# Attention beside a gated MLP on one core: which key tiles VectorE takes, and the lengths a build-time order is made from

## The chip, the core and the metric

One core of a Trainium2 chip runs the whole kernel. TensorE multiplies (its results land in PSUM, eight banks of 128 x 512 float32), ScalarE evaluates exp and gelu, VectorE and GpSimd work elementwise, and DMA queues move data between memory and the on-chip SBUF. Each engine executes its own list of instructions in order; where one needs another's result it waits for a semaphore. The metric is the device time of one execution in microseconds. Five executions of the kernel before took 743.12, 743.48, 743.58, 744.07 and 745.52 us, so the median is 743.58.

## The reference, cut to what matters

`x` has 2048 rows of 512. `a` is attention with 32 heads of width 16 that share one set of keys and values; `b` is a gated MLP whose second half is layer-normalised and multiplied by a 2048 x 2048 matrix. A sigmoid gate per row mixes them.

```
q = (x @ wq) as 32 heads of 16;  k = x @ wk;  v = x @ wv
p = softmax(q k^T * 0.25);       a = (p v, heads side by side) @ wo
z = gelu(x @ w_in);              z1, z2 = halves of z, 688 columns each
g = w_sp @ layernorm(z2) + b_sp; b = (z1 * g) @ w_out
out = s * a + (1 - s) * b,       s = sigmoid(sum(x * gate_w))
```

The costly part is the softmax: 32 heads x 2048 queries x 2048 keys are 134 million exponentials.

## The kernel before, in words

**Attention blocks.** The work on scores is cut into 32 units (`NU`). A unit is one chunk of 512 queries (there are four) with four heads, and has 16 key tiles of 128 keys; a block is one key tile of one head, a 128 x 512 tile of scores. So there are 32 x 16 x 4 = 2048 blocks, and each passes through one matmul on TensorE (`s_mm`, shown by the profile as `ps<-QA,KA`), an exponential, and one matmul with the values (`ps<-P,V` or `ps<-X,V`) that accumulates into one PSUM bank for the unit.

**Two engines make the exponentials.** ScalarE takes two blocks at a time: TensorE fills one of two pairs of banks (0 and 1, 2 and 3), and one ACTIVATE turns the 128 x 1024 scores into P (`exp_op`, L621). VectorE takes a whole key tile of a unit, four blocks, which the code calls a batch. It drains two blocks at a time from banks 4 and 5 with a linear map (`d_A`, L645, two drains for each batch), then squares the 128 x 2048 result twice (`d_square`, L657). The fourth power of a linear function stands in for exp, and what it misses is a linear function of the scores, which eight short matmuls for each unit put back (`cor_mm`, with the sums MC and CC made once by `g_MC`, L451). MC is built for the last 1, 2, ... up to `NMAX` = 7 key tiles, since a unit's VectorE tiles are taken from the end of its list of tiles. GpSimd does a share of the second square: up to two pieces of `GE` = 384 columns of a batch (`g_piece`, L664), and VectorE's second square is shorter by as much.

**The start.** x arrives transposed in four chunks of 512 rows. For each chunk, TensorE multiplies by wk (`g_K`, L357) and VectorE copies the keys out of PSUM (`k_ev`, L350); `g_V` (L412) makes values, the gate's sums and a second copy of the keys (L418 to L420). After the keys of the last chunk, four DMAs issued by GpSimd copy all keys to other partitions (`k_shift`, L352 to L354); units with an odd number need that copy. Key tile n belongs to chunk n // 4. In the kernel before, ScalarE goes through the key tiles 0, 1, 2, ... and VectorE takes 15, 14, 13, ...; so VectorE's first tile needs the last chunk of keys (`new_batch`, L791, asks for `("K", 0, 3)`).

**The rest.** The MLP (`g_z2`, `z1_mm`, `g_sp`, `g_fin`, `g_part`) fills what TensorE and VectorE have left between the attention steps; the gelus run on ScalarE in one stretch of their own, between two table loads. The groups of such matmuls share one PSUM bank (`BM`), which VectorE empties. At the end the last unit is normalised and four row tiles are written out (L1302 to L1311). `keep_pick` (L1045) puts matmuls whose result adds nothing where TensorE had little to do for 3.4 us.

**The order.** All of these instruction lists are made while the kernel is built, by a planner that plays the engines forward with a fixed length for each piece of work (`pe_pick` L854, `act_pick` L1110, `dve_pick` L1157, main loop from L1258). The lengths that matter here: `LAT` = 120 ns from an engine's end to what another sees of it, `EXPT` = 904 ns for an exp of two blocks, `C512` = 218 ns for a 512-column matmul, `SW` = 105 ns when TensorE changes from one kind of matmul to another, 226 ns for a step of scores. TensorE may begin a step of scores once the exp two steps back has ended and must begin it `SLATE` = 490 ns before the running exp ends (`dl`, L918); other matmuls are only placed if they end before that. A pair of blocks for VectorE is placed `LAT + DMARG` = 220 ns after the last drain has ended (`d_ok`, L838). The times decide only the order; on the chip the semaphores decide when things run.

```
ACT's blocks of a unit, in order:   order = [(n // 4, n % 4) for n in range(64)]
VectorE's next key tile:            un["hi"] -= DB;  batches.append((u, un["hi"] // 4))
latest begin of a step of scores:   dl = max(t, nxt - SLATE)
```

Of the kernel before, what the change touches and what calls it, by code (L numbers as in the profile page):

```python
# [17 lines left out]
DH = 16  # L18
# [12 lines left out]
K2MAX = 0.142  # L31
ZMAX = 25.0

NPB = 21
NX = 6
DB = 4
NQ = 4
NMAX = 7
# [4 lines left out]
DPQ = 3500.0  # L43
SOLO = 300.0
PJOIN = 1
APRI = 1.5
DMARG = 100.0
DRAW = 115.0
RIDE = 0.0
GE = 384  # L50
GLAT = 160.0
GNS = (60.0, 2.0)
EMARG = 50.0
EXPT = (0, 478, 904, 1330)
SLATE = 490.0
KEEP = 7.5
LOW = 6.5
MMARG = 120.0
# [109 lines left out]
def build_kernel(nc, x_d, wq_d, wk_d, wv_d, wo_d, win_d, wsp_d, bsp_d, wout_d, gw_d, out_d):  # L168
    es = ExitStack()
    with es:  # L170
# [22 lines left out]
        wvg = sb("wvg", [128, 4, 34], B16)  # L193
# [123 lines left out]
        BMK = ("bk", BM)  # L317
        T = {"now": 0.0}
        LAT = 120.0
        C512, C344 = 218.0, 148.0  # L320
        SW = 105.0
        C2 = 78 + 0.5208 * 256 * DB

        class Group:
# [87 lines left out]
        def g_V(c):  # L412
            def piece(k, dt):
                t0 = 512 * c + 128 * k
                return lambda: mm(bank(BM, 33, 64 * k), xT[:, dt, t0:t0 + 128], wvg[:, dt, 0:33], dt == 0, dt == 3,
                                  ["wv", "gw", "wvk", ("x", c)], [BMK], tag="V")
            src = bank(BM, 256).rearrange("p (k w) -> p k w", w=64)
            e1 = lambda: op("dve", lambda v: v.tensor_copy(V1[:, 4 * c:4 * c + 4, 0:DH], src[:, :, 0:DH]), r=[BMK], w=[("V", c)], tag="Vev")  # L418
            e2 = lambda: op("dve", lambda v: v.tensor_copy(gs[:, 4 * c:4 * c + 4].unsqueeze(2), src[:, :, 32:33]), r=[BMK], w=[("gs", c)], tag="gsev")
            e3 = lambda: op("dve", lambda v: v.tensor_copy(KT0[:, 4 * c:4 * c + 4, :], src[:, :, 16:32]), r=[BMK], w=[("KT0", c)], tag="ktev")  # L420

            def done(t):
                T[("V", c)] = t
                if c >= 2:
                    dve_q.append((600, lambda: op("dve", lambda v: v.tensor_copy(
                        Kt[:, 4 * (c - 2):4 * (c - 2) + 4, :].rearrange("p k (h d) -> p k h d", d=DH),
                        KT0[:, 4 * c:4 * c + 4, :].unsqueeze(2).broadcast_to([128, 4, 8, DH])), r=[("KT0", c)], w=[("Kt", c)], tag="Kt"), t, setT(("Kt", c))))
                if c == 3:
                    gate_and_k()
            def all_():  # L430
                for k in range(4):
                    for dt in range(4):
                        piece(k, dt)()
            return Group("V%d" % c, [(480, all_)], [(150, e1), (100, e2), (130, e3)],
                         lambda: when(("x", c)), done)

        def gate_and_k():
            t = T["now"] + 400
# [12 lines left out]
        def g_MC():  # L451
            pieces = []
            for h in range(2):
                for i in range(NMAX):
                    kt = 15 - i
                    pieces.append((90, lambda h=h, i=i, kt=kt: mm(
                        bank(BM, 32 * (NMAX - i), 256 * h + 32 * i).rearrange("p (n e) -> p n e", e=32),
                        Kt[:, kt - 8, :] if h == 0 else ones[:, 0:128], V1[:, kt, :].unsqueeze(1).broadcast_to([128, NMAX - i, 32]),
                        i == 0, i == NMAX - 1, [("Kt", kt // 4), ("V", kt // 4), "ones"], [BMK], tag="MC")))
            msrc = bank(BM, 32 * NMAX).rearrange("p (n e) -> p n e", e=32).unsqueeze(2).broadcast_to([128, NMAX, 8, 32])  # L460
            mk = mke[:].unsqueeze(1).unsqueeze(3).broadcast_to([128, NMAX, 8, 32])
            e1 = lambda: op("dve", lambda v: v.tensor_tensor(MC[:], msrc, mk, ALU.mult), r=[BMK, "mke"], w=["MC"], tag="MC")
            e2 = lambda: op("dve", lambda v: v.tensor_scalar(ct[:, 0, :], bank(BM, 32 * NMAX, 256), E0, None, ALU.mult), r=[BMK], w=["ct0"], tag="CC")
            cc = CC[:, :, :].rearrange("p n e -> p (n e)")
            e3 = lambda: op("dve", lambda v: v.tensor_copy(cc, ct[:, 0, :]), r=["ct0"], w=["CC"], tag="CC")
            e4 = lambda: op("dve", lambda v: v.tensor_tensor(ct[:, 1, :], ct[:, 0, :], cc, ALU.subtract), r=["ct0", "CC"], w=["ct1"], tag="CC")
            e5 = lambda: op("dve", lambda v: v.tensor_scalar(ct[:, 1, :], ct[:, 1, :], s01[:, 1:2], None, ALU.mult), r=["ct1", "s01"], w=["ct1"], tag="CC")
            e6 = lambda: op("dve", lambda v: v.scalar_tensor_tensor(cc, cc, s01[:, 0:1], ct[:, 1, :], ALU.mult, ALU.add), r=["CC", "ct1", "s01"], w=["CC"], tag="CC")
            def some(h):
                for c_, f_ in pieces[NMAX * h:NMAX * h + NMAX]:  # L470
                    f_()
            return Group("MC", [(500, lambda: some(0)), (500, lambda: some(1))], [(1950, e1), (320, e2), (320, e3), (320, e4), (250, e5), (320, e6)],
                         lambda: when(("Kt", 2), ("Kt", 3), ("V", 2), ("V", 3)), setT("MC"))

        def g_RH():

# [255 lines left out]
        op("dve", lambda v: v.tensor_scalar(s01[:, 0:1], pidx[:, 0:1], 0.0, None, ALU.is_equal), r=["pidx"], w=["s01"])  # L732
        op("dve", lambda v: v.tensor_scalar(s01[:, 1:2], pidx[:, 0:1], 1.0, None, ALU.is_equal), r=["pidx"], w=["s01"])

        for c in range(4):
            T[("x", c)] = 6300.0 + 4200.0 * c
        T[("K", 0, 0)] = 8000.0
        T[("Q", 0)] = 9000.0
        T["wq1"] = 9000.0
        T["win"] = 29000.0  # L740
        T[("wT", 0)] = 55000.0
# [21 lines left out]
        misc = {"cur": None, "free": 0.0}  # L763

        units = [{"lo": 0, "hi": 64, "left": 64, "cor": 0} for _ in range(NU)]
        order = [(n // 4, n % 4) for n in range(64)]
        st_ = {"ua": 0, "kf": 0, "ke": 0, "pu": 0, "pp": 0}
        stepb, sdone, edone = {}, {}, {-1: 0.0, -2: 0.0}
        pfree = [0.0] * NPB
# [21 lines left out]
        def new_batch(now):  # L791
            m = len(batches)
            if m >= NX and pd_left.get(m - NX, 0) > 0:
                return False
            ua = unit_for_act()
            for u in (ua, ua + 1):
                if u >= NU:
                    continue
                un = units[u]
                if un["hi"] - un["lo"] < (RMIN if u < NU - 1 else RLAST) + DB or un["hi"] <= 64 - 4 * NMAX:  # L800
                    continue
                if u > ua and un["hi"] <= 64 - PRE:
                    continue
                q = when(("Q", u // 2), ("K", 0, 3)) if u % 2 == 0 else when(("Q", u // 2), "K1")
                if q is None or q > now:
                    continue
                un["hi"] -= DB
                batches.append((u, un["hi"] // 4))
                pd_left[m] = DB
                cur["m"] = m  # L810
                cur["hs"] = [0, 1]
                return True
            return False
# [22 lines left out]
            return take  # L836

        def d_ok(now):  # L838
            return dpair["free"] is not None and dpair["free"] + LAT + DMARG <= now and sum(1145 if x[1] == "dW" else 2290 for x in polyq) <= DPQ

        class Done(dict):
            def get(self, k):
# [6 lines left out]
        edone = Done(edone)  # L849

        def sw(kind):
            return 0.0 if last_pe["kind"] == kind else SW

        def pe_pick(now):  # L854
            k = st_["kf"]
# [21 lines left out]
                    cands.append((t + (0 if ph["j"] else LAT), 0, C512 + sw("M"), emit_z, fin_z, "M"))  # L877
            elif ua < NU and edone.get(k - 2) is not None:
                bl = []
                t = edone[k - 2] + (LAT if k >= 2 else 0)  # L880
                u = ua
                lo = units[u]["lo"]
                while len(bl) < 2 and u < NU:
# [14 lines left out]
                if bl:  # L898
# [12 lines left out]
                        unit_for_act()  # L911

                    def fin(t_end):
                        sdone[k] = t_end + LAT
                        for x in new:
                            da_q.append((t_end + LAT + EMARG,) + x)
                    nxt = edone[k - 1] if edone.get(k - 1) is not None else edone[k - 2] + (EXPT[len(stepb[k - 1])] if k - 1 in stepb else 0)
                    dl = max(t, nxt - SLATE)  # L918
                    ride = dpair["end"] + LAT + DMARG
                    if max(now, t) < ride <= dl - RIDE and (cur["hs"] or new_ok(now)):  # L920
                        t = ride
                    cands.append((t, 0, sw("S") + 226, emit, fin, "S"))
            if d_ok(now) and (dl is None or ua >= NU or t > now + SOLO):
                tk3 = d_pair(now, ())
                if tk3:
                    new3 = []

                    def fin_d(t_end):
                        da_q.append((t_end + LAT + EMARG,) + new3[0])
                    cands.append((now, 1, sw("S") + 216, lambda: new3.append(tk3()), fin_d, "S"))  # L930
            elif dpair["free"] is not None and dpair["free"] + LAT + DMARG > now:
                cands.append((dpair["free"] + LAT + DMARG, 9, 0, None, None))

            pu = st_["pu"]
            if pu < NU:
# [102 lines left out]
                cands = [c for c in cands if c[3] is None or c[5] == "S" or c[1] == 0.5 or max(now, c[0]) + c[2] <= dl]  # L1038
            return cands

        last_pe = {"kind": ""}
        tl_state = {12: 0, 13: 0}
        tl_bank = {12: BM, 13: BD}

# [65 lines left out]
        def act_pick(now):  # L1110
# [8 lines left out]
            if ph["k0"] is not None and gel and st_["ke"] == ph["k0"]:  # L1119
                kind, i = gel[0]  # L1120
                t = now if kind == "z2" else zready.get(i)
                if t is not None:
                    c_ = (1294 if kind == "z2" else 904) + (1300 if (kind, i) == ("z2", 0) or len(gel) == 1 else 0)

                    def e1():
                        gel.popleft()
# [133 lines left out]
        while True:  # L1260
# [5 lines left out]
            if rdy:  # L1266
# [6 lines left out]
                tend[eng] = t_end  # L1273
                if eng == "pe":
                    last_pe["kind"] = c[5]
                heapq.heappush(events, t_end)
                heapq.heappush(events, t_end + LAT)
                if c[4]:
# [198 lines left out]
```

## Time and profile before

| | |
|---|---|
| median of five executions | 743.58 us (743.12 to 745.52) |
| the profiled execution | 745.25 us, span from first to last instruction 743.3 us |
| ScalarE busy | 723.6 us, 97% of the span |
| VectorE busy | 699.8 us, 94% |
| TensorE busy | 697.0 us, 94% |
| GpSimd busy | 295.8 us, 40% |
| exps of two blocks on ScalarE | 760 |
| drains on VectorE | 264, for 132 batches |

The span is what the trace covers; the device time has 1.95 us more around it. A row of the groups names the source line, engine and operation, the tile written and the tiles read, the shape and the count, then the busy time in us, the mean length of one in ns, the idle time of that engine just before them, and what ended most of it. Because consecutive instructions of ScalarE and VectorE overlap a little in the records, the distance from start to start is shorter than the length of one: 904 ns against 1209 ns for the exps.

### The profile page before, as it was taken

The numbers are of one execution on the slowest core, as the hardware profiler recorded it, in microseconds if no ns is written. First come the engines' busy times: TensorE is split into PE (matmuls) and PEld (weight loads), VectorE is DVE, ScalarE is ACT, GpSimd is POOL, SyncE is SP. The second block draws the span as 40 slices with busy tenths as digits, with TensorE's granted clock in tenths as the row PEclk, the third lists the DMA queues.
The fourth block names the chain that finished last, engine by engine and source line by source line (L and its number), as shares of the span: only waits on it lengthen the run. The fifth ranks groups of instructions, "written<-read, shape, count | busy, mean of one in ns | idle before, by whom it ended". The sixth has DMA issues, their size and how long they took to land.

```text
span 743.3 us, 14057 instructions
## 1 busy us (share of the span) xinstructions
PE 697.0 (94%) x5502; PEld 186.0 (25%) x5502; DVE 699.8 (94%) x803; ACT 723.6 (97%) x786; POOL 295.8 (40%) x305
## 2 busy tenths in 40 slices
PE   7989999999899999999999999999999999999996
PEld 2322222223322222222222222222222222222221
DVE  3699999999999999999999999999999999999996
ACT  5999999999899999999999999999999999999995
POOL 4234433333134534434234444434444443444441
PEclk9999999999989999999999999999999999999999
DMA  9810000000000000140000042000005000000001
GB/s 214 179 25 1 1 1 1 1 1 1 1 1 1 1 1 2 30 94 22 1 1 1 1 86 52 8 1 1 1 1 114 15 8 9 1 1 1 1 1 33
DMA packets 49114, 17.06 MB, mean 23 GB/s; under 512 B 44145, under 2 KB 48977, under 8 KB 49042
## 3 DMA queue, kind: packets, MB, share of 16 engines
q1 hardware_dynamic: 46130, 15.15, 9.3%
q10 hardware_dynamic: 2784, 0.69, 0.4%
q8 instruction: 45, 0.74, 0.4%
q0 software_dynamic: 128, 0.26, 0.2%
q14 instruction: 27, 0.22, 0.1%
HBM read 3.25 MB, written 2.10 MB: 7 GB/s over the span
## 4 chain that ended last, share of the span: by engine, by line
ACT 69%; issue 16%; PE 12%; DMA 1%; DVE 1%; ACTq 0%
ACT P L621 67%; PE ps L308 9%; PE ps L307 4%; ACT z L514 1%; DMA xT<-in_A_x_dram 1%; ACT z L518 1%; ACTq L156 0%; ACT L621 0%; ACT L518 0%; DVE outsb L1307 0%; DVE T L675 0%; DVE OT L690 0%; DVE KA L350 0%; ACT outsb L1310 0%; DVE sel L728 0%
## 5 line engine op out<-in xcount | busy, mean ns | idle before, releaser
L621 ACT ACTIVATE P<-ps 128x1024 bf16<-128x1024 f32 x760 | 697.6, 1209 | 2.1 <-PE ps L308 1.9
L308 PE MATMUL ps<-QA,KA 32*128 32x512 bf16 x2048 | 315.2, 386 | 36.3 <-ACT P L621 32.0
L645 DVE TENSOR_SCALAR X<-ps 128x1024 f16<-128x1024 f32 x264 | 321.1, 1216 | 17.4 <-PE ps L308 15.9
L664 POOL TENSOR_TENSOR X<-X 128x384 bf16<-128x384 f16 x190 | 157.5, 829 | 347.1 <-DVE X L657 245.1
L657 DVE TENSOR_TENSOR X<-X 128x2048 f16<-128x2048 f16 (+3 forms) x264 | 283.6, 1081 | 2.2
L308 PEld LDWEIGHTS ps<-QA,KA 32*128 32x128 bf16 x2048 | 76.2, 91 | 336.1 <-ACT P L621 326.3
L308 PE MATMUL ps<-P,V 128*32 128x512 bf16 x1520 | 138.6, 386 | 0.0
L681 POOL TENSOR_TENSOR rc<-T,mone 128x16 f32<-128x16 f32 x31 | 97.2, 3134 | 49.6 <-DVE T L675 48.3
L307 PE MATMUL ps<-wT,z 128*128 128x512 bf16 x320 | 99.0, 384 | 0.0
L308 PE MATMUL ps<-X,V 128*32 128x512 bf16 x528 | 65.2, 387 | 0.0
L308 PEld LDWEIGHTS ps<-P,V 128*32 128x32 bf16 x1520 | 28.8, 94 | 43.2 <-issue 41.8
L307 PEld LDWEIGHTS ps<-wT,z 128*128 128x128 bf16 x320 | 21.4, 97 | 43.6 <-issue 40.4
L307 PE MATMUL ps<-win,xT 128*128 128x344 bf16 x128 | 30.4, 314 | 0.1
L307 PE MATMUL ps<-wout,z 128*128 128x512 bf16 x96 | 29.7, 384 | 0.0
L675 DVE STREAM_TRANSPOSE T<-ps 128x512 f32<-128x512 f32 x32 | 22.7, 710 | 1.6 <-PE ps L308 1.3
L307 PE MATMUL ps<-wo,OT 128*128 128x512 bf16 x64 | 20.5, 384 | 0.5 <-DVE OT L690 0.5
L307 PE MATMUL ps<-xT,wq 128*128 128x512 bf16 x64 | 20.6, 385 | 0.2 <-DVE RHO L481 0.2
L307 PE MATMUL ps<-ones 128*128 128x512 bf16 x51 | 18.3, 455 | 2.4 <-DVE ones L251 1.5
L687 POOL TENSOR_TENSOR Tn<-T,rcg 128x256 bf16<-128x256 f32 x31 | 19.3, 622 | 2.4
L307 PE MATMUL ps<-xT,win 128*128 128x512 bf16 x80 | 18.8, 380 | 0.9 <-ACT z L514 0.8
L308 PEld LDWEIGHTS ps<-X,V 128*32 128x32 bf16 x528 | 15.2, 94 | 16.9 <-issue 14.7
L508 DVE CAST z<-ps 128x344 bf16<-128x344 f32 x32 | 16.2, 507 | 0.4 <-PE ps L307 0.2
(113 smaller groups left out, 288.0 us busy)
## 6 DMA issues: line engine op xcount, KB each, us to landing
out_dram<-outsb SPq DMA_DIRECT2D x15, 128.0 KB, 1.7
win<-in_B_w_in_dram SPq DMA_DIRECT2D x2, 688.0 KB, 6.9
wout<-in_B_w_out_dram SPq DMA_DIRECT2D x1, 640.0 KB, 9.3
wo<-in_A_wo_dram SPq DMA_DIRECT2D x1, 512.0 KB, 8.0
wq<-in_A_wq_dram ACTq DMA_DIRECT2D x1, 384.0 KB, 7.2
wT<-in_B_w_sp_dram SPq DMA_TRANSPOSE x16, 4.5
KA<-KA POOLq DMA_DIRECT2D x4, 64.0 KB, 2.9
wq<-in_A_wq_dram ACTq DMA_DIRECT2D x1, 128.0 KB, 4.0
```

The source lines that it names most:

```text
L307: return t.matmul(dst, lhsT, rhs, start=start, stop=stop)
L308: return t.matmul(dst, lhsT, rhs, start=start, stop=stop, tile_position=tp)
L508: ev = lambda: op("dve", lambda v: v.tensor_copy(z2[:, FH * st + 344 * h:FH * st + 344 * h + 344], bank(BM, 344)), r=[BMK], w=[("z2", st)] ...
L514: op("act", lambda a: a.activation(z1[:, 1024 * i:1024 * i + 1024], bank(b, 1024), ACT.Gelu_apprx_tanh), r=[bkey(b), bkey(b + 1)], w=[("z1 ...
L518: op("act", lambda a: a.activation(z2[:, 2 * k * FH:2 * (k + 1) * FH], z2[:, 2 * k * FH:2 * (k + 1) * FH], ACT.Gelu_apprx_tanh), r=[("z2", ...
L621: op("act", lambda a: a.activation(P[:, 512 * p:512 * (p + n)], ps[:, 512 * b0:512 * (b0 + n)], ACT.Exp), r=[bkey(b0 + i) for i in range(n ...
L645: op("dve", lambda v: v.tensor_scalar(X[:, m % NX, 1024 * h:1024 * h + 1024], bank(BD, 1024), PA, PB, ALU.mult, ALU.add), r=[bkey(BD), bke ...
L657: op(eng, lambda v: v.tensor_tensor(x if tag == "dU" else x.bitcast(B16), x, x, ALU.mult), r=ks, w=ks, tag=tag)
L664: op("pool", lambda g: g.tensor_tensor(x.bitcast(B16), x, x, ALU.mult), r=ks, w=ks, after=[pg.ops["dve"][-1]], tag="gW")
L675: o("dve", lambda v: v.transpose(T1[:], bank(BO)), r=[("bk", BO)], w=["T1"], tag="T1")
L681: o("pool", lambda g: g.tensor_tensor(rc[:].unsqueeze(2), lsum, mone[:].unsqueeze(2), ALU.pow), r=["T1", "mone"], w=["rc"], tag="rc")
L687: o(e, lambda v: v.tensor_tensor(tn, t1[:, :, 0:16], s_[:].unsqueeze(2).broadcast_to([128, 16, 16]), ALU.mult), r=["T1", k], w=[("Tn", pr, ...
```

## The change

- A list `KL` gives the order of the key tiles: 0, 1, 2, 4, 5, 8, 9, 12, 13, 6, 10, 14, 15, 11, 7, 3. ScalarE goes through it from the front, VectorE from the back. So VectorE takes 3 (first chunk), 7 (second), 11 (third), 15 (fourth), then 14, 10, 6. `new_batch` asks for the chunk of the tile itself and no longer for the fourth. Kt, the copy of the keys that `g_MC` needs, is made for two tiles of each of the four chunks (128 x 256, four times) and not for four tiles of the last two (128 x 512, twice).
- GpSimd's pieces have 416 columns and not 384.
- The planner's lengths change. Seen by TensorE, a bank is free 60 ns (`FREE`) after the exp or drain that reads it, and no longer 120; a pair for VectorE is placed 110 ns after a drain and no longer 220. Seen by ScalarE and VectorE, scores are there 204 ns (`SEEN`) after the step, and no longer 120 and 170. An exp of two blocks counts 917 ns and not 904, a matmul 221 and not 218, a change of kind 103 and not 105, and the latter only as far as TensorE was not idle. A step of scores must begin 535 ns before the running exp ends, and no longer 490. The arrivals of the chunks of x are put at 6.3, 10.7, 14.2 and 17.2 us and no longer at 6.3, 10.5, 14.7 and 18.9.

```diff
+KL = (0, 1, 2, 4, 5, 8, 9, 12, 13, 6, 10, 14, 15, 11, 7, 3)
...
-DMARG = 100.0
+DMARG = 50.0
...
-GE = 384
+GE = 416
...
-EXPT = (0, 478, 904, 1330)
-SLATE = 490.0
+EXPT = (0, 491, 917, 1343)
+SLATE = 535.0
+FREE = 60.0
+SEEN = 204.0
...
-        C512, C344 = 218.0, 148.0
-        SW = 105.0
+        C512, C344 = 221.0, 150.0
+        SW = 103.0
...
-                if c >= 2:
-                    dve_q.append((600, lambda: op("dve", lambda v: v.tensor_copy(
-                        Kt[:, 4 * (c - 2):4 * (c - 2) + 4, :].rearrange("p k (h d) -> p k h d", d=DH),
+                dve_q.append((330, lambda: op("dve", lambda v: v.tensor_copy(
+                    Kt[:, 2 * c:2 * c + 2, :].rearrange("p k (h d) -> p k h d", d=DH),
...
-                    kt = 15 - i
+                    kt = KL[15 - i]
...
-        order = [(n // 4, n % 4) for n in range(64)]
+        order = [(KL[n // 4], n % 4) for n in range(64)]
...
-                q = when(("Q", u // 2), ("K", 0, 3)) if u % 2 == 0 else when(("Q", u // 2), "K1")
+                q = when(("Q", u // 2), ("K", 0, KL[un["hi"] // 4 - 1] // 4)) if u % 2 == 0 else when(("Q", u // 2), "K1")
...
-                batches.append((u, un["hi"] // 4))
+                batches.append((u, KL[un["hi"] // 4]))
...
-            return dpair["free"] is not None and dpair["free"] + LAT + DMARG <= now and sum(1145 if x[1] == "dW" else 2290 for x in polyq) <= DPQ
+            return dpair["free"] is not None and dpair["free"] + FREE + DMARG <= now and sum(1145 if x[1] == "dW" else 2290 for x in polyq) <= DPQ
...
-            return 0.0 if last_pe["kind"] == kind else SW
+            return 0.0 if last_pe["kind"] == kind else max(0.0, last_pe["end"] + SW - T["now"])
...
-                t = edone[k - 2] + (LAT if k >= 2 else 0)
+                t = edone[k - 2] + (FREE if k >= 2 else 0)
...
-                        sdone[k] = t_end + LAT
+                        sdone[k] = t_end + SEEN
```

In the instruction lists of the changed kernel, ScalarE has 752 exps (760 before), VectorE 272 drains and 272 squares (264 and 264 before): 136 first squares of 2048 columns, then 72 second squares of 1216 columns, 43 of 1632 and 21 of 2048 (75 of 1280, 40 of 1664 and 17 of 2048 before). GpSimd has 187 pieces (190 before). TensorE has the same 2048 blocks of scores, and 114 matmuls of `keep_pick` and the warm-up where there were 91. VectorE's first drain stands ahead of the copies of the first chunk's values, behind the square of the first queries (L372).

## The prediction

> **What bounds the kernel now.** I read the page's busy times first, then its costliest groups, then busy times by stretch, then the timeline where it matters.
>
> ```profile
> PE 697.0 (94%) x5502; PEld 186.0 (25%) x5502; DVE 699.8 (94%) x803; ACT 723.6 (97%) x786; POOL 295.8 (40%) x305
> ...
> L621 ACT ACTIVATE P<-ps 128x1024 bf16<-128x1024 f32 x760 | 697.6, 1209 | 2.1 <-PE ps L308 1.9
> L645 DVE TENSOR_SCALAR X<-ps 128x1024 f16<-128x1024 f32 x264 | 321.1, 1216 | 17.4 <-PE ps L308 15.9
> L664 POOL TENSOR_TENSOR X<-X 128x384 bf16<-128x384 f16 x190 | 157.5, 829 | 347.1 <-DVE X L657 245.1
> L657 DVE TENSOR_TENSOR X<-X 128x2048 f16<-128x2048 f16 (+3 forms) x264 | 283.6, 1081 | 2.2
> ```
>
> ScalarE is the bound (97%), with VectorE and TensorE close: its 760 exps have 2.1 us of idle before them. The same row hides waits, since records overlap: in the trace the exps start 904 ns apart in 564 of 757 intervals, never less, but 918.8 on average. The excess is 11.2 us: 0.6 in the first 40 us, 1.7 in two intervals at 205 to 209 us, 8.9 in the other 717.
>
> ```profile
> core 0: us, PE busy (x) PEld busy (x) DVE busy (x) ACT busy (x) POOL busy (x), PEclk, DMA share, GB/s
> 10.00:24.50 14.50, 12.54 (x95) 3.62 (x96) 3.25 (x11) 14.36 (x16) 0.47 (x1) 1.00 1.12 275
> 24.50:175.50 151.00, 138.02 (x1160) 39.16 (x1160) 147.79 (x183) 150.99 (x166) 58.99 (x62) 1.00 0.07 15
> 175.50:209.25 33.75, 30.77 (x177) 11.08 (x175) 32.36 (x64) 30.42 (x31) 8.36 (x7) 0.92 0.00 0
> 209.25:733.60 524.35, 503.90 (x4017) 127.96 (x4015) 507.50 (x527) 524.35 (x572) 220.15 (x220) 1.00 0.08 16
> ```
>
> Exps begin at 9.91 us and end at 733.6; 9.7 us of normalising and output follow. VectorE idles 11.25 us before its first drain (24.55), and 21.45 from there to 733.6.
>
> ```profile
> 400.64 3.10 ACT L621 ACTIVATE P<-ps 128x1024 bf16<-128x1024 f32 x3
> 401.05 0.39 PE L308 MATMUL ps<-QA,KA 32*128 32x512 bf16 x4
> 401.37 0.82 PE L307 MATMUL ps<-wT,z 128*128 128x512 bf16 x3
> 402.13 0.39 PE L308 MATMUL ps<-QA,KA 32*128 32x512 bf16 x2
> ```
>
> Here is one of the late intervals. The third exp starts at 402.56 and not 402.45. Three MLP matmuls stand before its scores, which begin at 402.13: 430 ns ahead of the exp. Ahead of all 54 exps that come over 50 ns late in the long stretches, and hold 6.5 of the 8.9 us, the distance is 429 or 430. The old order thinks 226 + 120 = 346 enough; 226 + 204 = 430 is what the new one counts.
>
> [...] The trace has 904, so 904 is used. [...] the trace has 1216, and 1134 from start to start. [...] pieces beside drains take 829 ns, one beside a square (205.19) took 1.20 us.
>
> **The change part by part.**
>
> *Eight exps less.* 8 x 904 = 7.2 us off ScalarE's path. Four batches move to VectorE.
>
> *VectorE's price.* From start to start the trace has 1134 for a drain, 1142 for a first square, and 745, 932 and 1145 for second squares of 1280, 1664 and 2048 columns; the slope of 0.52 ns per column gives 711 for 1216 and 915 for 1632. Before: 264 x 1.134 + 132 x 1.142 + 75 x 0.745 + 40 x 0.932 + 17 x 1.145 = 562.7. After: 272 x 1.134 + 136 x 1.142 + 72 x 0.711 + 43 x 0.915 + 21 x 1.145 = 578.3. That is 15.6 us more. Kt costs nothing extra: four copies at an estimated 200 against two at 290. The cover is idle time: between 10 us and the last exp VectorE worked 723.6 - 32.7 = 690.9, so now 706.5, which can't end before 716.5. ScalarE's own floor is 9.9 + 752 x 0.904 + 24.8 (gelu stretch, 175.53 to 200.36) + 0.1 = 714.7. So both are near their floor, and VectorE's is the higher.
>
> *The early drain.* The square L372 starts at 10.01 and lets go at 10.34; the first drain then follows. Of the 11.25 idle us some 10 become useful, and the unit's ScalarE exps drop from 30 to 26.
>
> *What the drain delays.* The copies of keys (L350) queue behind drains on VectorE, and TensorE's pairs for VectorE (banks 4 and 5) stand ahead of key matmuls. I walk VectorE's new list with lengths from start to start: drain 1.13, first square 1.14, key copy 0.60, a chunk's three value copies 0.45, Kt 0.20. First drain 10.34 to 11.47, values and Kt to 12.1, second drain to 13.25, square to 14.45, keys of chunk 1 out at 15.05 (14.1 before). ScalarE has six exps from chunk 0 in the new order; the seventh can't start before 15.15 + 0.43 = 15.58, 0.25 after the sixth's end. Then second square to 15.98, third drain to 17.1, keys of chunk 2 to 17.7, fourth drain to 18.85, values to 19.3, square to 20.45, fifth drain to 21.6, Kt and second square to 22.5, sixth drain to 23.65, and only then the keys of chunk 3, out at 24.25. The fifteenth exp needs them and would be due at 22.8; it starts near 24.8. In all 2.2 us of waiting, where before the two long distances at 10.8 and 27.4 us lost 0.6. Net 1.6 against the change; bounds: 0, if that copy is ready sooner, and 3. On GpSimd three pieces now stand ahead of the key DMAs (L354), 0.9 us each and started beside earlier drains, so done by then; the DMAs land at 24.25 + 5.1 = 29.4 (23.73 to 28.82 before), when the odd unit's first pair is due: no further wait. No other DMA moves.
>
> *Lengths.* 535 in place of 490 asks for scores 45 ns earlier. Capping each of the 717 intervals' excess at 45 removes 4.9 us. Against it: drains are asked for 110 ns sooner, so a late drain blocks TensorE and the scores behind. The trace shows few such waits (TensorE's weight loads waited for L645 9 times, 2.6 us in all). Bounds: 8.9 off, and nothing. I take 3.5 off, because VectorE's idle time must at the same time fall from 32.7 to some 8 us.
>
> *Fillers and pieces.* 23 matmuls of 0.216 are 5 us of TensorE, beside 38 us idle between 10 and 733.6; without that cover they would delay scores. 416 columns are an estimated 829 x 416/384 = 898 ns on GpSimd, inside the 1134 of a drain, so free; GpSimd is 40% busy. The tail has the same steps: one exp, its value matmuls, transposes, last products, output; 9.7 stays.
>
> *Sum.* -7.2 + 1.6 - 3.5 = -9.1. The profiled execution took 745.25, 1.95 beyond its span and 1.7 above the median; it would become 736.1. Taken from the median: 734.5. VectorE then idles 8.0 us before the last exp's end at 724.5.
>
> **The rivals.**
>
> *The late scores stay.* The new order spaces exps by 917, the mean distance in the long stretch before is 916 (523.3 us from 209.25 to 732.5, 571 intervals). If the execution keeps that spacing, only the count pays: 743.6 - 7.2 + 1.6 = 738.0. For it: VectorE's floor. Against: late scores have a plain cause that is changed.
>
> *The late scores go.* 738.0 - 8.9 = 729.1, or up to 732 with some left. For it: TensorE's shorter planned latency and 38 us of room. Against: VectorE would be left with 3 us idle.
>
> *Slower: drains hold TensorE up.* Each of 272 pairs may find its banks still being drained, since 220 ns of margin became 110; TensorE is in order, so the next scores wait too. Place: `d_ok` and the drain's pair. It decides from 9.1 / 272 = 33 ns a pair on average passed on to exps; at 50 ns it gives 734.5 + 13.6 = 748. Against: MLP copies take VectorE less than the order allows (the transposes L675 710 ns long, 632 from start to start, counted 716), so VectorE is rather early.
>
> *It does not do what it says.* The instruction lists show the drain ahead of the first values and 752 exps; only the use of the early time could fail, which is the first rival.
>
> **How the numbers follow.** Forecast 734.5 with own range 732.5 to 736.5: 0.46. Late scores stay, 736.5 to 741: 0.26. They go, 729 to 732.5: 0.18. Slower, above 745: 0.06. Within 0.2% of before (1.5 us, about what can be told from no change): 0.04. So faster 0.90, same 0.04, slower 0.06. Range 730 to 740: it takes in the first two rivals save their ends, and both bounds of the start.
>
> **What would show it.** Right: 752 exps, 904 as the commonest distance, excess in the long stretches near 5.4; first drain near 10.3; a hole of about 2 us in ScalarE near 23 to 25, ended by K3's copy; VectorE's idle time below 10 us from 10 us on. Wrong: TensorE's waits for L645 far above 2.6 us (the slower rival); excess of 8 or more (first rival); no hole at the start, or one of 5 us; the tensor clock below 1 in a further stretch, as it fell to 0.92 from 175.5 to 209.25.

## The result, and the profile after

The changed kernel takes 743.41 us (median of 42 executions, 739.34 to 750.16). The kernel before took 744.78 beside it (79 executions, 742.9 to 751.69). The ratio is 0.9984, with a 95% interval from 0.9969 to 0.9998: a gain of about 0.2%, where 9 us (1.2%) were forecast. The predicted 734.5 and the range 730 to 740 miss it.

The executions differ by the tensor clock: 1 means that TensorE was granted its full clock throughout. Of 44 recorded ones of the changed kernel 7 have a mean clock of 0.997 or more and take 739.34 to 740.75; 36 are below 0.996. At 0.986 it takes 745 to 748. The profiled one (744.05 us, span 742.2, clock 0.991) is typical. The page first:

```profile
PE 699.1 (94%) x5525; PEld 191.7 (26%) x5525; DVE 710.2 (96%) x821; ACT 717.9 (97%) x778; POOL 305.7 (41%) x302
...
L625 ACT ACTIVATE P<-ps 128x1024 bf16<-128x1024 f32 x752 | 691.9, 1125 | 7.2 <-PE ps L313 6.8
...
L649 DVE TENSOR_SCALAR X<-ps 128x1024 f16<-128x1024 f32 x272 | 330.5, 1215 | 9.2 <-PE ps L313 7.8
L668 POOL TENSOR_TENSOR X<-X 128x416 bf16<-128x416 f16 x187 | 164.7, 881 | 345.3 <-DVE X L661 278.1
L661 DVE TENSOR_TENSOR X<-X 128x2048 f16<-128x2048 f16 (+3 forms) x272 | 290.1, 1074 | 1.5
```

The parts of the change are there: eight exps fewer, eight drains more, VectorE's idle time before drains 9.2 us where it was 17.4. The exps' own idle time has risen from 2.1 us to 7.2. Busy time by stretch says where, with the same columns as before (busy time of PE, PEld, DVE, ACT and POOL, then the granted clock):

```profile
10.00:24.50 14.50, 12.50 (x112) 4.21 (x111) 14.43 (x24) 12.64 (x14) 2.75 (x4) 1.00 1.12 280
24.50:175.50 151.00, 138.29 (x1130) 40.03 (x1127) 143.98 (x181) 146.47 (x159) 59.12 (x60) 0.97 0.08 15
175.50:209.25 33.75, 29.21 (x191) 10.41 (x188) 32.10 (x73) 31.80 (x33) 9.46 (x6) 1.00 0.00 1
209.25:733.00 523.75, 507.83 (x4055) 133.53 (x4054) 510.94 (x526) 523.32 (x571) 226.62 (x216) 1.00 0.08 16
```

VectorE works 14.43 of the first 14.5 us (3.25 before): the early drain is used. ScalarE loses 1.9 us there and 4.5 us in the second stretch, where the clock is 0.97. The timeline of ScalarE shows the holes; the number in brackets is the idle time before the group.

```profile
24.57 3.77 ACT L625 ACTIVATE P<-ps 128x1024 bf16<-128x1024 f32 x4 [1.45 <-PE ps L313]
...
32.86 1.02 ACT L625 ACTIVATE P<-ps 128x1024 bf16<-128x1024 f32 x1 [1.67 <-PE ps L313]
...
36.09 1.02 ACT L625 ACTIVATE P<-ps 128x1024 bf16<-128x1024 f32 x1 [0.92 <-PE ps L313]
37.60 3.18 ACT L625 ACTIVATE P<-ps 128x1024 bf16<-128x1024 f32 x3 [0.49 <-PE ps L313]
```

The hole at 24.57 is the 15th exp, which waits for the last key copy (L355, 23.40 to 24.09). That was forecast. The one at 32.86 was not. TensorE's timeline just before it:

```profile
29.41 0.39 PE L313 MATMUL ps<-QA,KA 32*128 32x512 bf16 x3
31.57 0.39 PE L313 MATMUL ps<-QA,KA 32*128 32x512 bf16 x1 [1.76 <-DMA KA<-KA]
```

TensorE stands at the odd unit's first VectorE pair until the fourth key DMA has landed. The row of that DMA's line says how long the four took:

```profile
DMA to landing us min/median/max: 2.4/2.5/5.5
```

They are issued at 24.39, 25.10, 25.59 and 26.06 us. The second transposing load of wT is issued at 25.77 on SP's queue, just ahead of the fourth, which lands at 31.52. In the kernel before, the second wT load came at 26.11, behind all four, and the slowest took 3.1 us. Then the clock:

```profile
30.00:34.00 4.00, 2.43 (x22) 1.12 (x22) 1.95 (x3) 2.21 (x3) 0.55 (x1) 0.86 0.43 57
34.00:38.00 4.00, 4.00 (x25) 0.58 (x21) 3.86 (x7) 2.45 (x3) 0.00 (x0) 0.50 0.55 118
38.00:42.00 4.00, 4.00 (x23) 0.95 (x22) 2.59 (x5) 3.62 (x4) 0.42 (x1) 0.50 0.58 131
```

TensorE works 2.43 of 4 us, and then runs at half its clock for some 10 us (8 in the last two rows; the 0.86 of the first row, and again from 42 to 46, means half the clock for 1.1 us of four): busy without a break, ScalarE waiting. The recorded clock is halved from 32.91 to 43.15 us, which is 10.24 us or three times 3.41. In the profile of the kernel before it is halved from 204.00 to 210.83, which is 6.83 us or twice 3.41. The 3.41 us ahead of the fall (29.50 to 32.91) were not idle: TensorE was busy for 48% of them.

**Reading the pace of exps anew.** The prediction measured exps from start to start: 904 ns as the pace, and all above it as lateness. Two views of the changed kernel's ScalarE show the error. First single exps, with start and length in us, then the ten from the first to the second (shortest, median and longest in ns, first and last start):

```profile
319.28 1.07 ACT L625 ACTIVATE P<-ps 128x1024 bf16<-128x1024 f32 x1
...
327.42 1.19 ACT L625 ACTIVATE P<-ps 128x1024 bf16<-128x1024 f32 x1
```

```profile
L625 ACT ACTIVATE P<-ps x10: 1072/1128/1185, 319.3 to 327.4; 128x1024 bf16<-128x1024 f32 x10
```

Starts are 904 ns apart, but each record is some 13 ns longer than the one before. The ends are (327.42 + 1.185 - 319.28 - 1.072) / 9 = 917 ns apart. The next exp starts 1025 ns on, which the prediction calls 121 late, but its end comes 917 after the last one: nothing was lost. In the kernel before, ends are 916 to 918 ns apart nearly everywhere, and all waits beyond 917 in its long stretches (46 to 177 and 212 to 734 us) come to 0.20 us. The 8.9 us of late scores never existed.

Measured by ends, the time of the profiled executions goes like this (us; an exp counts 0.9166, the mean of ends without a wait):

| | before | after | difference | predicted |
|---|---|---|---|---|
| end of the first exp | 10.94 | 10.45 | -0.49 | 0 |
| other intervals of exps (758, 750) | 694.78 | 687.45 | -7.33 | -7.2 |
| interval with the gelus | 25.87 | 25.87 | 0 | 0 |
| waits until 46 us | 0.47 | 7.74 | +7.27 | +1.6 |
| waits after | 1.76 | 1.36 | -0.40 | -3.5 |
| last exp to the end of the span | 9.51 | 9.37 | -0.14 | 0 |
| span | 743.3 | 742.2 | -1.1 | -9.1 |

Of the 7.74 us until 46, some 0.8 are small waits up to 22 us, 1.55 the hole for the last keys, 1.78 the key DMA, and 3.6 the half clock after it.

### The profile page after: what moved, and what is told of

Its sections match the earlier page's. It is cut to its first block, busy times and chain, and to the rows that moved or that the text cites. A ratio compares the mean times of both kernels' runs of the same rounds, so it can differ in the third digit from the quotient of the medians.

```text
span 742.2 us, 14106 instructions
## 1 busy us (share of the span) xinstructions
PE 699.1 (94%) x5525; PEld 191.7 (26%) x5525; DVE 710.2 (96%) x821; ACT 717.9 (97%) x778; POOL 305.7 (41%) x302
## 3 DMA queue, kind: packets, MB, share of 16 engines
HBM read 3.25 MB, written 2.10 MB: 7 GB/s over the span
## 4 chain that ended last, share of the span: by engine, by line
ACT 60%; issue 18%; PE 17%; DVE 2%; POOL 1%; DMA 1%; ACTq 0%; POOLq 0%
ACT P L625 58%; PE ps L313 12%; PE ps L312 5%; ACT z L518 1%; DVE X L649 1%; DMA KA<-KA 1%; ACT z L522 1%; DVE X L661 1%; POOL bspz L264 0%; POOL KA L261 0%; DVE KA L355 0%; ACTq L161 0%; POOL KA L359 0%; ACT L625 0%; ACT L522 0%
## 5 line engine op out<-in xcount | busy, mean ns | idle before, releaser
L313 PE MATMUL ps<-QA,KA 32*128 32x512 bf16 x2048 | 319.1, 386 | 33.3 <-ACT P L625 25.7
L649 DVE TENSOR_SCALAR X<-ps 128x1024 f16<-128x1024 f32 x272 | 330.5, 1215 | 9.2 <-PE ps L313 7.8
L668 POOL TENSOR_TENSOR X<-X 128x416 bf16<-128x416 f16 x187 | 164.7, 881 | 345.3 <-DVE X L661 278.1
L661 DVE TENSOR_TENSOR X<-X 128x2048 f16<-128x2048 f16 (+3 forms) x272 | 290.1, 1074 | 1.5
L313 PEld LDWEIGHTS ps<-QA,KA 32*128 32x128 bf16 x2048 | 78.4, 91 | 318.7 <-ACT P L625 288.0
L313 PE MATMUL ps<-X,V 128*32 128x512 bf16 x544 | 67.5, 386 | 0.0
L691 POOL TENSOR_TENSOR Tn<-T,rcg 128x256 bf16<-128x256 f32 x31 | 22.3, 719 | 2.4
L312 PE MATMUL ps<-ones 128*128 128x512 bf16 x60 | 20.9, 426 | 1.5 <-DVE ones L256 1.5
L312 PE MATMUL ps<-ones,zeros 128*128 128x512 bf16 x54 | 20.6, 403 | 0.0
L313 PEld LDWEIGHTS ps<-X,V 128*32 128x32 bf16 x544 | 15.9, 94 | 17.3 <-issue 14.6
```

The source lines that it names most:

```text
L312: return t.matmul(dst, lhsT, rhs, start=start, stop=stop)
L313: return t.matmul(dst, lhsT, rhs, start=start, stop=stop, tile_position=tp)
L649: op("dve", lambda v: v.tensor_scalar(X[:, m % NX, 1024 * h:1024 * h + 1024], bank(BD, 1024), PA, PB, ALU.mult, ALU.add), r=[bkey(BD), bke ...
L661: op(eng, lambda v: v.tensor_tensor(x if tag == "dU" else x.bitcast(B16), x, x, ALU.mult), r=ks, w=ks, tag=tag)
L668: op("pool", lambda g: g.tensor_tensor(x.bitcast(B16), x, x, ALU.mult), r=ks, w=ks, after=[pg.ops["dve"][-1]], tag="gW")
L691: o(e, lambda v: v.tensor_tensor(tn, t1[:, :, 0:16], s_[:].unsqueeze(2).broadcast_to([128, 16, 16]), ALU.mult), r=["T1", k], w=[("Tn", pr, ...
```

## The experiments

Where a sentence below says "at full clock", it takes the executions with a mean clock of 0.997 or more; the kernel before has 55 of those among its 120 executions beside these runs, 742.8 to 745.3 with 743.3 in the middle. Waits are counted by ends of exps, beyond 917 ns, in the profiled execution.

**The wT loads behind the key DMAs.**

```diff
-        ld_wT(0)
...
-            for g in range(4):
-                dma("pool", ...Ksh...)
+            sh = [dma("pool", ...Ksh...) for g in range(4)]
+            ld_wT(0, sh)
```

> The changed kernel, except that the first load of wT (on SP's queue) waits until the four DMAs that copy the keys to other partitions have landed; all instruction lists are otherwise the same. Theory (the start eats the gain): in the changed kernel the fourth key DMA landed at 31.5 us, 5.5 us after its issue, because the second transposing load of wT had been issued 0.3 us ahead of it; TensorE stood 1.8 us at the pair of an odd unit behind it, then ran at half clock from about 34 to 42 us. Then here all four land within 3 us of issue (by 29.5), TensorE has no wait for them above 0.3 us, the clock stays at 1.00 from 30 to 46 us, exps up to 46 us lose under 4 us and not 8.0, and the kernel takes 3.5 to 5 us less than the changed one: 738 to 740. Rival (the key copy behind the drains is what costs): only the 1.8 us of waiting for the DMA goes, the clock still falls after the hole at 23 us, and under 2 us are gained.

739.34 us (738.76 to 744.59, 7 executions), ratio 0.9932 (0.9896 to 0.9969). The fourth key DMA lands at 28.49, and TensorE doesn't stand:

```profile
30.00:34.00 4.00, 3.88 (x44) 1.29 (x36) 3.93 (x5) 4.00 (x6) 0.54 (x1) 1.00 0.58 132
34.00:38.00 4.00, 3.55 (x30) 1.08 (x30) 3.93 (x8) 3.86 (x5) 0.19 (x1) 1.00 0.58 131
```

Waits until 46 us fall from 7.74 to 2.93. The clock stays 1.00 there in the profile, and six of seven executions have a mean of 0.998 or more, where the changed kernel had 7 of 44 at 0.997 or more. So moving the loads gained 4 us in the median. At full clock the middle is 739.21 against 739.85, so nearly all of the gain is the clock. How many executions of the changed kernel have the collision isn't shown: the second wT load is issued when the first has landed, at 25.77 us in the profile above, but at 27.06, 29.42 and 29.84 in those of three other versions with the loads unmoved (below: tile 6, exp of 904, odd unit later). The fourth key DMA takes 5.46 us with a wT load issued 0.29 us ahead of it in the changed kernel, and 2.44 here without; in the run `before_lite` below, a wT load 0.35 us ahead again goes with 5.32.

**Each half of the change alone:** `KL` and Kt with the old lengths, and the new lengths with the old order of tiles.

> The order of the key tiles KL, with Kt as in the change, but all lengths, GpSimd's 384 columns and the arrival times as in the kernel before. Its lists hold 758 exps and 266 drains. Theory (start): the keys of chunk 3 are copied behind drains and the odd unit's pair stands as early as in the change, so the start loses 4 us or more and the late scores of the long stretches stay near 9 us: count -1.8, start +4, so 745 to 748, slower than before. Rival (the lengths are what hurts): the tiles by themselves are harmless and give 741 to 743.

> All new lengths, 416 columns and arrival times, but key tiles in the old order (ScalarE 0, 1, 2, ..., VectorE 15, 14, ...) with the old Kt. Its lists hold 758 exps and 266 drains. Theory: without early drains the start is as before (under 1 us lost up to 40 us), the count gives -1.8, and the late scores are as many as in the changed kernel (12 to 15 ns an exp, about 10 us), so 742 to 744. What the prediction held (asking for scores 45 ns sooner takes late scores away): late scores of 5 to 6 us, 738 to 740.

The tiles alone: 748.76 us (17 executions), ratio 1.004 (1.0015 to 1.0065), 745.08 to 745.97 at full clock. 758 exps, a hole of 2.26 us for the last keys, and the first exp ends at 11.95, since the value matmuls stand ahead of the first scores and wait for gate_w. (The change also has the planner count gate_w as there only at 9.7 us, which puts the scores first; this run takes that back.) The lengths alone: 744.16 (14 executions), ratio 0.9997 (0.9964 to 1.0029); 758 exps. That is where the theory put it; two exps and the 3.5 us that the prediction gave to the lengths would be 5.3 less, and the interval ends at 2.7. Each half removes only two exps, both together eight.

**An exp counted 904 in the changed kernel,** all else as changed.

> The changed kernel, but the planner counts an exp of two blocks at 904 ns again (gelu too). Its lists hold 754 exps and 270 drains. Theory (late scores follow the spacing of the order): steps that hold eight value matmuls and one more matmul between two steps of scores need over 904 ns; an order at 917 allows them, one at 904 allows fewer, so the late scores of the long stretches fall from 10 us to 6 to 8, and the time is 1 to 3 us below the changed kernel if the start is alike. Rival (it is the load, not the spacing): late scores stay at 10 us or more and the time rises by the two exps, 1.8 us.

746.36 us (22 executions), ratio 1.0007 (0.9982 to 1.0032), 740.58 to 741.34 at full clock; 754 exps. This and the next two runs were meant to find why the late scores had stayed. By starts, the excess over 904 stays at 9 to 11 us in all of them, which no theory of spacing explained; that is how the records came into doubt.

**A bank counted as free 300 or 310 ns after its exp,** in the kernel with the wT loads moved.

```diff
+EFREE = 300.0
...
-                t = edone[k - 2] + (FREE if k >= 2 else 0)
+                t = edone[k - 2] + (EFREE if k >= 2 else 0)
```

> The kernel with the wT loads behind the key DMAs (739.34 us), and in it a time of its own for an exp's banks: the planner lets TensorE begin a step of scores 300 ns after its end of the exp two steps back, where it had 60. In the trace a score begins at best 1264 ns after the start of the exp that read its banks (1209 of record and 55), and the planner's exp of 917 with 60 makes that 977. So the planner's window between the earliest and the latest begin of a score is 382 - 60 = 322 ns wide, and the chip's is 474 - 360 = 114: an MLP matmul with eight value matmuls (1188 ns from scores to scores) fits the first (917 + 322 = 1239) and not the second (904 + 114 = 1018), and every one comes late by up to 170 ns. With 300 the planner's window is 82 wide: such steps go (28 + 16 + 11 before, 4 in this list), three MLP matmuls (1074 ns, 46 of them) stay and lose about 50 ns each. Theory (the window's left edge makes the late scores): late time in the long stretches falls from 9.6 us to 4 to 5, two exps less take 1.8, so 739.3 - 5 - 1.8 = 732.5, between 730.5 and 735. Rival (TensorE is simply full: 930 ns of busy time an exp): the work only moves, the late time stays at 8 to 10 us, 736.5 to 740.

> As the run with 300 ns, with 310: the planner's window is then 72 ns wide and three MLP matmuls between two score steps no longer fit either (9 left of 46); exps 750 in both. Theory: late time in the long stretches 1.5 to 3 us, 2 less than with 300. But 148 MLP matmuls and transposes then stand in the last sixteenth of the score steps where 95 stand with 300 and 62 with 60, so work of 53 x 0.22 = 12 us is pushed to the end, where some of it may come after the last exp: if TensorE's room is the limit, the gain is given back there and the time is 733 to 737 with a tail over 11 us; if not, 728.5 to 733. Rival (TensorE is full everywhere): late time as before, 736.5 to 741.

With 300: 740.25 us (11 executions), 737.71 to 738.06 at full clock. Of 55 steps that were to go 4 are left in the list, yet the excess of starts stayed at 9 us, and the theory fell. What did change is two exps: 739.34 - 1.83 = 737.5. With 310: 753.23 us (6 executions). Its ScalarE is done as early as with 300 (last end 725.56 and 725.35), but then 26.3 us follow, where 10.6 follow with 300: the planner found no place for the MLP's products and left them to the end. TensorE's room is a bound after all, at the tail. And its trace has a long stretch of equal records:

```profile
L623 ACT ACTIVATE P<-ps x38: 1345/1345/1345, 397.6 to 431.5; 128x1024 bf16<-128x1024 f32 x38
```

Here starts are (431.5 - 397.6) / 37 = 0.916 us apart. The scores come as early as their banks allow: TensorE waits each time for the exp two back to end, and the next exp starts 0.49 us after that end. Each record lasts 1345 ns, where the shortest of this run lasts 1019, so no exp ends late for want of scores. 917 ns is ScalarE's pace, by starts too. (The longest record of the kernel before lasts 1347 ns, that of the changed kernel 1305.)

**Less work on TensorE.** Two runs left out 14 of 16 matmuls of each product with w_sp, in the order otherwise unchanged, one of them in the kernel before:

> The kernel before with 14 of the 16 matmuls of each product with w_sp left out (392 matmuls, 73 us of TensorE; b is then wrong), in the same order of everything else. It tests what the distance of exps is made of. Ends of exps stand 916 to 918 ns apart in the kernel before nearly everywhere, and only 0.2 us in the long stretches is more than that; starts stand 904 apart, each record 13 ns longer than the one before it, until a score that comes 430 ns ahead of its exp resets it. Theory (ScalarE's own pace is 917 ns, the records of starts drift): no gain, 743.5 to 745, and ends 917 apart as before. Rival (the prediction: the pace is 904 and late scores cost 8.9 us): the late starts have far less cause, 4 us or more off, 737 to 741.

807.81 us (6 executions), and the other, on the better kernel below, 794.93. With 73 us less to do, TensorE's clock fell to a mean of 0.82 in both profiles, so these times told nothing of the pace. A third let the planner fill:

> Tile 6 moved and wT behind the key DMAs (736.95 us), with 14 of the 16 matmuls of each product with w_sp left out (b is then wrong), but TensorE kept busy by the planner's own fillers: 143 more of them for 392 left out, 42 us of TensorE less; the run without them had its clock at half for much of the time, so it could not tell. 754 exps. Theory (ScalarE's pace is 917 ns from end to end, and where scores are early enough from start to start too): 736.95 + 1.83 = 738.8, between 738 and 740, with more starts 917 apart and longer records. Rival (the pace is 904 and late scores cost 8 to 9 us): fewer late scores, 4 us or more off, 734.8 or less.

759.42 us (6 executions): neither theory's time, since the MLP's last products again come after the last exp (731.94; 25.4 us follow) and the clock is at 0.984. But where the clock is full the pace can be read. Between 260 and 400 us, first in the same kernel with all matmuls (tile 6 and the wT loads moved, below) and then with the omission:

```profile
260.00:400.00 140.00, 131.56 (x1061) 35.70 (x1071) 138.75 (x143) 139.95 (x154) 57.65 (x58) 1.00 0.08 20
```

```profile
260.00:400.00 140.00, 122.89 (x1012) 31.06 (x1004) 136.67 (x139) 140.00 (x154) 62.40 (x59) 1.00 0.09 20
```

TensorE's idle time doubles, from 8.4 to 17.1 us, and 154 exps are touched in both. Ends are 917.0 ns apart with the omission (918.8 without). At 904 it would be two exps more.

**Tile 6 for ScalarE,** first with the wT loads moved, then with them where the change leaves them:

```diff
-KL = (0, 1, 2, 4, 5, 8, 9, 12, 13, 6, 10, 14, 15, 11, 7, 3)
+KL = (0, 1, 2, 4, 5, 6, 8, 9, 12, 13, 10, 14, 15, 11, 7, 3)
...
-NMAX = 7
+NMAX = 6
```

> The kernel with the wT loads behind the key DMAs (739.34 us), and in it key tile 6 moved from VectorE's seventh place to ScalarE's sixth (the correction is built for six tiles and not seven; no unit takes more). ScalarE then needs the last chunk of keys at its 17th exp and not at its 15th, 1.8 us later, by when VectorE has copied it out. Theory (the hole of 1.45 us at 24.6 us is that copy and nothing else): the hole goes, about 1.4 us less, 738.0 (736.8 to 739). Rival (the order of the rest decides, or another wait takes the place of the hole): no change within 1 us, or slower, since the order has 56 steps of the kind that comes late where it had 55.

> The changed kernel with tile 6 moved from VectorE's seventh place to ScalarE's sixth (the correction is built for six tiles), and the wT loads where they were. So the hole of 1.55 us that waits for the last key copy goes, and TensorE's stop at the fourth key DMA may stay. It tells which of the two brings the half clock that most executions have. Theory (either idle time can bring it, and the DMA's alone is enough): as the changed kernel without the hole, 741 to 743.5, the clock below 0.996 in more than half of the executions. Rival (the hole at 25 us brings it, as in the run with the odd unit later, where nothing waited for the DMA and 6 of 14 executions still had a clock of 0.982 or less): near 737.5 to 739, clock at 0.997 or more in nearly all.

736.95 us (736.78 to 737.26, 6 executions), ratio 0.9893 (0.9859 to 0.9927): the lowest median of all. And 737.07 (736.73 to 741.3, 8 executions), ratio 0.99 (0.9865 to 0.9934), with the loads unmoved, its waits until 46 us 0.66 in place of 7.74:

```profile
24.00:30.00 6.00, 5.48 (x80) 2.33 (x79) 4.58 (x18) 6.00 (x9) 2.15 (x4) 1.00 0.85 168
30.00:34.00 4.00, 3.86 (x32) 1.31 (x31) 3.83 (x6) 4.00 (x5) 0.88 (x1) 1.00 0.28 64
34.00:38.00 4.00, 3.74 (x41) 1.16 (x39) 3.80 (x7) 4.00 (x6) 0.74 (x1) 1.00 0.58 131
```

ScalarE works without a hole. In this order the odd unit's first pair stands behind 23 pairs of ScalarE and not 21, and TensorE comes to it at 29.95, when the key DMAs have landed (29.65). But the second wT load was issued at 27.06 here, behind all four, so this profile has no collision. The theory, which expected the clock below 0.996 in more than half of the executions, is refuted (6 of 8 are at full clock); what a collision would do without the hole is not shown.

With tile 6 and the wT loads moved, a bank counted as free after 300 ns gives 750 exps:

> Tile 6 moved, wT behind the key DMAs, and a bank counted as free 300 ns after its exp: 750 exps. Theory (the time is the number of exps by 917 ns and the waits at the start, as long as VectorE and TensorE have room): 736.95 - 1.83 = 735.1, between 734.5 and 736. Rival (VectorE, with a batch more and 13 us of idle time after 40 us, or TensorE is the bound by now): no gain, 736.9 or more.

740.62 us (22 executions), ratio 0.9946 (0.9917 to 0.9974). The two exps are gone, but 6.1 us of waits stand at 43.4 to 49.4 us, where this order puts the next queries' matmuls so late that the exps of a new unit wait for them, and the clock is at half for some 3 of these us. The planner's order decides more than two exps do.

**The odd unit planned later, and the kernel before with wT moved.**

```diff
-                    T["K1"] = t + 4500
+                    T["K1"] = t + 8500
```

> The changed kernel with one number of the planner changed: the shifted keys are counted as there 8.5 us after the last key copy and not 4.5, so the odd unit's first pair stands behind 24 pairs of ScalarE and not 21, 2.7 us later; the wT loads stay where they were. The order has 754 exps (752). Theory (TensorE's stop at the fourth key DMA, and the half clock after it, cost the changed kernel 4 us): that DMA may land as late as before, but nothing waits for it; ends from 30 to 46 us lose under 1 us where they lost 5.3, the clock is 0.996 or more in most executions, and the time is 739.3 + 1.8 for two exps = 741, between 740 and 742. Rival (the half clock has another cause, TensorE's idling at the start as such): 743.5 to 746.

> The kernel before, with only the order of the DMAs changed: the transposing loads of wT wait until the four key DMAs have landed. In the kernel before these landed by 28.82 us and no score waited for them. Theory (the landing cost time only because the changed kernel's fourth key DMA is issued behind the second wT load): no gain here, 743.5 to 745.5. Rival (wT's loads disturb the start in both kernels): 1.5 us or more faster, 743 or less.

Later: 742.95 us (14 executions), ratio 0.9972 (0.9933 to 1.0012). At full clock 740.28 to 740.85, as the theory had it, but that is 5 executions; 6 have a clock of 0.982 or less. In the profiled one nothing waits for the DMA, and the clock is at half from 27 to about 50 us:

```profile
24.00:30.00 6.00, 4.88 (x55) 1.71 (x55) 4.86 (x18) 4.85 (x6) 2.15 (x4) 0.74 0.95 139
30.00:34.00 4.00, 4.00 (x27) 1.71 (x26) 0.49 (x2) 2.65 (x4) 0.00 (x0) 0.50 0.64 135
```

So the clock fell after the hole for the last keys alone. With the wT loads moved, the least busy 3.4 us have 57% too, and the clock stayed in the profile. Stretches of 3.41 us, counted from the times at which each trace's clock changes, show a difference. First the changed kernel's stretch ahead of its fall, then that of this run, then two stretches with the wT loads moved:

```profile
29.50:32.91 3.41, 1.65 (x16) 0.48 (x17) 1.01 (x2) 1.74 (x3) 0.88 (x1) 1.00 0.55 61
```

```profile
23.47:26.88 3.41, 1.93 (x27) 0.75 (x26) 3.37 (x7) 2.03 (x3) 2.27 (x5) 1.00 1.28 195
```

```profile
21.64:25.06 3.42, 2.64 (x31) 1.14 (x30) 3.42 (x5) 1.98 (x3) 1.55 (x2) 1.00 0.36 119
25.06:28.47 3.41, 2.71 (x33) 0.90 (x32) 2.38 (x11) 3.41 (x6) 1.47 (x4) 1.00 0.46 77
```

In the first two, one stretch has the whole idle time: TensorE is busy for 48% and 57% of it, and the clock fell at its end. In the third trace, the hole is shared by two stretches, with 77% and 79%, and the clock stayed. That the place of such stretches in an execution decides what a hole costs is a guess from these three traces and not shown: one run's clock (`key6_bank300`) fell after a stretch with 83%.

The kernel before with wT moved: 745.06 (14 executions), ratio 1.0012 (0.9989 to 1.0036), no gain, as expected; the loads don't collide in the profile of the kernel before. Its own profiled execution (751.04 us) runs at half clock from 13.02 to 36.92 us, with neither the early drains nor the collision; so neither of them brought the clock down there.

## Why the prediction was wrong, step by step

*Eight exps less: right.* -7.33 us against -7.2.

*VectorE's price: right in kind.* The records of drains and squares add up to 15.9 us more (15.6 predicted), but they overlap more: VectorE's busy time from 10 us to the last exp's end rose from 690.9 to 701.5, and its idle time fell only from 32.9 to 21.4, where 8.0 was predicted. And the floors were in the wrong order. With 917 in place of 904, ScalarE alone needs 10.45 + 687.45 + 25.87 = 723.8 us, above VectorE's 716.5. ScalarE stayed the bound, as the first rival's spacing said.

*The early drain: right.* It starts at 10.34.

*What the drain delays: right up to the copy, then wrong.* Keys out at 24.09 (24.25 predicted), the 15th exp at 24.57 (24.8), a hole of 1.55. The step that failed is "the DMAs land at 24.25 + 5.1 = 29.4 [...] no further wait. No other DMA moves". The 5.1 was taken from the kernel before, with no look at what else was in the DMA engines. The wT load, issued 0.34 us sooner in this profile than in that of the kernel before, stood ahead of the fourth. TensorE's stop cost 1.78 us at once, and the half clock after it 3.6. Net 7.3 where 1.6 with a bound of 3 stood; a clock below 1 was named only among the signs, with no price.

*Lengths: wrong from the ground.* -3.5 was to come out of 8.9 us that starts seemed to lose. By ends the long stretches had 0.20 to lose; the changed kernel has 1.30 there. The prediction saw that the mean distance was 916 and that the new order counts 917, and put it to the planner's caution. It was the engine's pace. Its first rival used the right number for another reason, VectorE's floor.

*Pieces and tail: right* (a piece took 881 ns, 898 estimated; 9.37 us after the last exp, 9.51 before). That the fillers cost nothing fits the 1.30 us of waits in the long stretches. *Not seen:* the first exp ends 0.49 sooner, since the value matmuls no longer stand ahead of the first scores; and the dip of the clock at 204 to 211 us is gone in this profile, 1.5 us less.

*The slower rival* is not what happened: TensorE's weight loads wait 4.5 us for drains in all (2.6 before), far from the 9.1 that it needed.

With the two failed steps put right, the sum is -7.3 for the exps, -0.6 for the first exp and the tail, +1.1 for the long stretches, and at the start +1.9 without the key DMA's stop and +3.7 with it: -4.9 or -3.1. At full clock the middle of the 7 executions is 739.85, against 743.3: -3.5. The rest of the way to -1.4 is the clock. What stays open is what brings it down in the executions that were not profiled. The kernel before is at full clock in 55 of 120, the changed one in 7 of 44, with the wT loads moved in 6 of 7 (5 of 11 with a bank free after 300 ns), with tile 6 moved in 12 of 14 (two versions). So the hole and the loads seem to matter, but the kernel before, with neither hole nor collision in its profile, loses the clock often too. The DMA alone was not tried.

## What to carry to other kernels

Take an engine's pace from the ends of its records, or from a run of equal records, before calling anything late: where starts run ahead (here 904 ns apart, with ends 917 apart), records grow (13 ns each) and a "late" start only sets them back. When work is moved to an early stage, list every DMA in flight then and what is issued within a microsecond of those that something waits for (here 0.29 us ahead of one, which landed after 5.46 us). And price an idle stretch of TensorE by what its clock may do next, which in the profiled execution cost twice the stretch itself (3.6 us after 1.78).

## What the hardware showed unexpectedly

- An exp of 128 x 1024 from PSUM takes 917 ns from end to end, not 904; its record is 1017 to 1347 ns long in the kernel before and 1017 to 1305 in the changed one.
- The tensor clock was halved for 10.24 us in the changed kernel's profile, for 6.83 in that of the kernel before and for 23.89 in that of `before_shift`: three, two and seven times 3.41. It fell after 3.41 us in which TensorE was busy for 48% (changed kernel), 57% (`k1_late`) and 83% (`key6_bank300`); where a hole was shared by two such stretches (77% and 79%, `shift_first`), it stayed. In the changed kernel's profile TensorE was busy for all of the 10.24 us, and the clock was back only at their end.
- Less work was slower: 392 matmuls left out made the kernel before 63 us slower (807.81 beside 744.96), with a mean clock of 0.82 in the profile.
- The fourth SBUF-to-SBUF DMA of keys landed in 2.44 us with no transposing load issued just ahead of it (`shift_first`), and in 5.46 and 5.32 where one of another queue was issued 0.29 and 0.35 us ahead (the changed kernel, `before_lite`).
